# Opening of a fused adaLN, attention and GLU kernel: order of the modulation, activation and key weight loads, and of the products on them

## The chip, the cores and the metric

The kernel runs on one core of a Trainium2 chip. Its engines run side by side, each through its own list of instructions in order: TensorE (PE; its weight loads are shown apart as PEld), VectorE (DVE), ScalarE (ACT), GpSimd (POOL) and SyncE (SP). Loads and stores are issued as DMAs, here mostly from SP's queue and a few from ScalarE's, and all are carried by 16 DMA engines. The metric is device time in microseconds for one execution, as the median of several runs. The profile comes from one further execution with the hardware profiler.

## The reference

One block of a transformer on x of 2048 x 512, with a condition vector c of 512:

```python
mod = (_silu(c) @ w_mod).reshape(c.shape[0], 6, 1, -1)
sa, ca, ga, sb, cb, gb = (mod[:, 0], mod[:, 1], mod[:, 2], mod[:, 3], mod[:, 4], mod[:, 5])
h = _layernorm(x, axis=-1) * (1 + ca) + sa
x = x + ga * _A_ref(h, A_wq, A_wk, A_wv, A_wo, A_beta)
h = _layernorm(x, axis=-1) * (1 + cb) + sb
x = x + gb * _B_ref(h, B_w_gate, B_w_up, B_w_down)
```

`_A_ref` is attention with 32 heads of 16 over four segments of 512 rows: a softmax inside each segment, and a linear memory (`M`, `z`) that is carried from one segment to the next. `_B_ref` is a bilinear GLU with a hidden width of 1376. Everything is float32.

## The kernel before

The rows of x are taken in four segments of 512, each in four tiles of 128 rows (t). The 512 columns are four blocks of 128 (d or k). PE multiplies in a rounded float32 format, so each operand is split into a high part and a low part (names end in H and L), and a product is made of three: high by high, low by high, high by low. Splitting takes an operation on ScalarE or VectorE for the high part and a subtraction on VectorE or GpSimd for the low part.

The change lies in the opening, before the first attention scores. What happens there:

- **Condition.** `s_c` gets c (line 628, on SP's queue), ScalarE takes an exponential (`e`, line 670), and three small VectorE operations make the gate silu(c). `be` is beta, loaded on ScalarE's queue.
- **x.** `xload(0)` loads four tiles (`x`, line 643). The generator `ln` makes statistics on VectorE (`ast`, `amv`), a reciprocal root with ScalarE (`asd`, `ay`), normalises the four tiles in place (VectorE, `x<-x,amv,ay`), transposes them on PE into four banks (`atp`, one for each d), and then for each d scales and shifts with the modulation on ScalarE (`ahf`) and splits (`ahH`, `ahL`). For d = 0 and 2 the high part is made on VectorE (a cast), for d = 1 and 3 on ScalarE; all low parts are VectorE's.
- **Modulation.** `w_mod` columns for shift and scale (sa, ca) are loaded as eight blocks of 256 KB: `wm0_load(j)` loads half j of the columns for the four blocks k of the condition. Half 0 serves d = 0 and 1, half 1 serves d = 2 and 3. `mod0(j)` multiplies the four blocks of a half by the gate on PE (`m<-s_c,wm`; 16 matmuls in the program, which the trace shows as 32 records), and `mod0_out(j)` copies the result to `modc` on VectorE. The `ahf` of d = 0, 1 waits for the first copy, that of d = 2, 3 for the second.
- **Warm-up.** `warm(n)` issues n matmuls on zeros (`wups<-wu`), so that PE is at work before its data is there. `wu` is filled by VectorE.
- **Weights.** `load_g` loads the key or query weights of a group of eight heads (`wrk`, `wrq`) and splits them; `load_v` does so for the value weights (`wrv`). For the first group the high part is made on ScalarE, the low part on VectorE.
- **Projections.** `a_kq(0, 0, "k")` and `a_kq(0, 0, "q")` make the key and query products of the first group, 12 matmuls each (`kps`, `qps`). They are generators that pause after every third matmul, and the code alternates between them: six of one, six of the other for the blocks k = 0, 1, and then for k = 2, 3 as the activation blocks come in. The value products (`vps`) follow.

Order is written by hand: PE's instructions are chained in the order of the calls (`MM`, `TP`), a call of `pin` ties another engine's instruction or a DMA behind the last PE instruction of the program order for the scheduler, and the objects `CV` and `CA` chain VectorE and ScalarE in the opening. Loads on SP's queue stand in the order of their calls. Each DMA gets one of eight completion counters in turn, those issued from ScalarE's queue included, and it waits for the DMA that used its counter before.

The lines that drive the opening (1100 on):

```python
lw = [load_g("k", wk_, 0), load_g("q", wq, 0), load_v()]
next(lw[0])
wm0_load(1)
next(lw[1])
next(lw[2])
lng = ln(pa, pa, xts.pop(0), 0, ca_c, sa_c, "a", ("h", 8, 2), True)
next(lng)
mod0(0)
next(lng)
mod0_out(0, mp0[0])
mod0(1)
```

Of the kernel before, what the change touches and what calls it, by code (L numbers as in the profile page):

```python
# [8 lines left out]
F32 = mybir.dt.float32  # L9
# [8 lines left out]
P = 128  # L18
S, D, H, DH, NSEG, L, F = 2048, 512, 32, 16, 4, 512, 1376
KT = D // P  # L20
# [37 lines left out]
def tile_kernel(ctx, tc, x, wq, wk_, wv, wo, beta, w_gate, w_up, w_down, c, w_mod, out):  # L58
    nc = tc.nc
# [3 lines left out]
    def open_pool(**kw):  # L63
        p = tc.tile_pool(**kw)
        return p, p.__enter__()
# [13 lines left out]
    def pin(i):  # L79

        if last_pe[0] is not None:
            tc.add_manual_dep(i.ins, last_pe[0].ins.name, NOSYNC, reason="order")

    def MM(*a, **k):
        return pe(nc.tensor.matmul(*a, **k))  # L85
# [31 lines left out]
    def flush():  # L117

        while later:
            later.pop(0)()  # L120
# [36 lines left out]
    s_c = cst.tile([P, KT], F32, name="s_c")  # L157
# [9 lines left out]
    def rows(s, t):  # L167
        return slice(s * L + t * P, s * L + (t + 1) * P)
# [80 lines left out]
    apool, ap = open_pool(name="ap", bufs=1)  # L249
    PT = 6  # L250
# [374 lines left out]

    pwpool, pw = open_pool(name="pw", bufs=1, reuse_waits="tile")
    papool, pa = open_pool(name="pa", bufs=2, reuse_waits="tile")
    nc.sync.dma_start(s_c, c)
    wm = w_mod.rearrange("(k p) n -> p k n", p=P)

    def load_mod(i):
# [7 lines left out]
    def xload(s):  # L639
        xt = []  # L640
        for t in range(4):
            a = pa.tile([P, D], F32, tag="x", name=f"x{s}_{t}", bufs=4)
            pin(nc.sync.dma_start(a, x[rows(s, t), :]))
            xt.append(a)
        return xt

    xts = {0: xload(0)}
    NWU = 20
    wu = pa.tile([P, 512], BF, tag="rl", name="wu", bufs=1)
    vec.memset(wu, 0.0)  # L650
    wups = psp.tile([P, 2, 512], F32, tag="lk", name="wups", bufs=1)
# [1 line left out]
    def warm(n):  # L653
        for i in range(n):
            MM(wups[:, 0], wu[:, 0:P], wu, start=True, stop=True)

    warm(NWU)
    wm0 = []
    for k in range(KT):
        a = ap.tile([P, 2, 2, 256], F32, tag="pt", name=f"wm0_{k}", bufs=PT)  # L660
        wm0.append(a)

    def wm0_load(j):
        for k in range(KT):
            pin(nc.sync.dma_start(wm0[k][:, j], wm[:, k, :].rearrange("p (i c) -> p i c", c=D)[:, 0:2, 256 * j:256 * j + 256]))

    wm0_load(0)
    r0 = [[a[:, j].rearrange("p i c -> p (i c)") for a in wm0] for j in range(2)]
    nc.scalar.dma_start(be, beta[None, :].to_broadcast([P, H]))
    act.activation(e1, s_c, AF.Exp, scale=-1.0)  # L670
# [45 lines left out]
        CV.tensor_copy(sa_c[:, 2 * j:2 * j + 2], ps[:, 0:2])  # L716
        CV.tensor_scalar_add(ca_c[:, 2 * j:2 * j + 2], ps[:, 2:4], 1.0)

    def mod0(j):
        ps = mp0[j].rearrange("p (i n) -> p i n", n=P)[:, :, 0:MW]  # L720
        for k in range(KT):
            for i in range(4):
                MM(ps[:, i], r0[j][k][:, i * P:(i + 1) * P], s_c[:, k:k + 1].to_broadcast([P, MW]),
                   start=k == i == 0, stop=k == KT - 1, skip_group_check=True)
# [18 lines left out]
    wH, wL = {}, {}  # L743
# [3 lines left out]
    def staged(nm):  # L747
        tg, n = stage[nst[0] % len(stage)]
        nst[0] += 1
        return (ap if tg == "memb" else pa).tile([P, D], F32, tag=tg, name=f"wr{nm}", bufs=n)  # L750

    def load_g(nm, w, g):

        A, V = CA if g < 2 else act, CV if g == 0 else nc.gpsimd
        raw = staged(f"{nm}{g}")
        hi = wH[nm, g] = pw.tile([P, KT, P], F32R, tag=f"w{nm}H{g}", name=f"w{nm}H{g}", bufs=1)
        lo = wL[nm, g] = pw.tile([P, KT, P], F32R, tag=f"w{nm}L{g}", name=f"w{nm}L{g}", bufs=1)
        pin(nc.sync.dma_start(raw.rearrange("p (k c) -> p k c", c=P),
                              w.rearrange("(k p) n -> p k n", p=P)[:, :, g * P:(g + 1) * P]))
        yield  # L760
        hi, lo = (a.rearrange("p k (d h) -> p k h d", h=HG) for a in (hi, lo))
        raw = raw.rearrange("p (k h d) -> p k h d", k=KT, h=HG)
        pin(A.activation(hi, raw, AF.Copy))
        V.tensor_sub(lo, raw, hi.bitcast(F32))
        yield

    def load_v():
        raws = []
        for k in range(KT):
            wH["v", k] = pw.tile([P, D], F32R, tag=f"wvH{k}", name=f"wvH{k}", bufs=1)  # L770
            wL["v", k] = pw.tile([P, D], F32R, tag=f"wvL{k}", name=f"wvL{k}", bufs=1)
            raws.append(staged(f"v{k}"))
            nc.sync.dma_start(raws[k], wv[k * P:(k + 1) * P, :])
        yield
        for k in range(KT):
            CA.activation(wH["v", k], raws[k], AF.Copy)
            CV.tensor_sub(wL["v", k], raws[k], wH["v", k].bitcast(F32))
            yield
# [20 lines left out]
    def a_kq(s, g, nm):  # L799

        hH, hL = hcur[0]
        ph = phs.setdefault((s, g), {})
        if True:
            dst = kd if nm == "k" else qd
            ps = bank(f"{nm}ps{s}_{g}")
            n = 0
            three = ((wH, hH), (wH, hL), (wL, hH)) if s == 0 and g < 2 else ((wH, hH), (wL, hH), (wH, hL))
            terms = [(k, *ab) for k in range(KT) for ab in three]
            if s == 0 and g == 1:
                terms.sort(key=lambda t: t[1] is wL)  # L810
# [12 lines left out]
            A.activation(q3[:, i0, :], f, AF.Copy)  # L823
            V.tensor_sub(r, f, q3[:, i0, :])

            def rest():
                (CV.tensor_copy if fast else act.copy)(q3[:, i1, :], r)
                V.tensor_sub(q3[:, i2, :], r, q3[:, i1, :])
                nc.sync.dma_start(dst[s][g].rearrange("r p t -> p r t"), q3)

            if fast:
                rest()
            phi = (nm == "k" and s < NSEG - 1) or (nm == "q" and s > 0)
            if phi:
                if fast:
                    yield 0.0
                if nm == "q" and g > 0:
                    yield from drain()
                e = pa.tile([P, L], F32, tag="ph", name=f"ph{nm}{s}_{g}", bufs=3)
                if behind or after:  # L840
                    settle()
                rl = pa.tile([P, L], F32, tag="rl", name=f"rl{nm}{s}_{g}", bufs=1)
                ph[nm] = e

                def feature():
                    for a, fn in ((rl, AF.Relu), (e, AF.Exp)):
                        i = (CA if fast else act).activation(a, f, fn)
                        if lastex[0] is not None:
                            tc.add_manual_dep(i.ins, lastex[0].ins.name, NOSYNC, reason="order")

                def feature2():
                    pin((CV if fast else vec).scalar_tensor_tensor(e, e, 1.0, rl, op0=ALU.min, op1=ALU.add))
# [26 lines left out]
    def drain():  # L879
        while memq:  # L880
            w = mem_step()
            if w is not None:
                yield w
# [214 lines left out]
            credit[0] -= (mem_step() if len(key) == 3 and memq else next(fa)) or 0.0  # L1098

    lw = [load_g("k", wk_, 0), load_g("q", wq, 0), load_v()]  # L1100
    next(lw[0])
    wm0_load(1)
    next(lw[1])
    next(lw[2])
    lng = ln(pa, pa, xts.pop(0), 0, ca_c, sa_c, "a", ("h", 8, 2), True)
    next(lng)
    mod0(0)
    next(lng)
    mod0_out(0, mp0[0])
    mod0(1)  # L1110
    next(lw[0])
    next(lng)
    next(lng)
    mod0_out(1, mp0[1])
    next(lw[1])
# [433 lines left out]
    for f, tag in ((0, "bh7"), (1, "bl7"), (LAST, "bh4")):  # L1549
        a = pc.tile([P, 2, L], F32, tag=tag, name=f"q0_{f}", bufs=1)  # L1550
# [53 lines left out]
    for n in range(NU):  # L1604
        p, nm, i = units[n]
# [69 lines left out]
```

## Time and profile before

| what | us |
|---|---|
| median of 3 runs | 855.8 |
| lowest and highest run | 855.62, 856.07 |
| the profiled execution, its own time | 855.95 |
| its span in the trace | 854.2 |
| PE busy / VectorE busy / ScalarE busy | 835.8 / 642.2 / 498.0 |
| PE idle in the span (854.2 - 835.8) | 18.4 |

The granted clock of PE is 1.00 throughout. In a timeline each row is a start, a duration, the engine, the line, the operation with the tiles it writes and reads, and, in brackets, how long the engine was idle before it and what ended that. "SPq" and "ACTq" are DMA issues on these queues: their duration is that of the issue, not of the transfer. Line 39 and line 85 are helpers through which most operations of the opening go, so the tile's name tells one from another. A matmul's duration reaches past the start of the next one, since they are pipelined: what one costs in a row of many is the distance between starts.

### The profile page before, as it was taken

The numbers are of one execution on the slowest core, as the hardware profiler recorded it, in microseconds if no ns is written. First come the engines' busy times: TensorE is split into PE (matmuls) and PEld (weight loads), VectorE is DVE, ScalarE is ACT, GpSimd is POOL, SyncE is SP. The second block draws the span as 40 slices with busy tenths as digits, with TensorE's granted clock in tenths as the row PEclk, the third lists the DMA queues.
The fourth block names the chain that finished last, engine by engine and source line by source line (L and its number), as shares of the span: only waits on it lengthen the run. The fifth ranks groups of instructions, "written<-read, shape, count | busy, mean of one in ns | idle before, by whom it ended". The sixth has DMA issues, their size and how long they took to land.

```text
span 854.2 us, 14419 instructions
## 1 busy us (share of the span) xinstructions
PE 835.8 (98%) x4982; PEld 598.2 (70%) x4982; DVE 642.2 (75%) x1796; ACT 498.0 (58%) x759; POOL 276.2 (32%) x423
## 2 busy tenths in 40 slices
PE   9989999999999999999999999999999999999998
PEld 6756656666665656656665677887888778888886
DVE  7897768887778967787888359999987855447554
ACT  4758767787676876677545626344445546455230
POOL 2756627566565764675434600000000000000000
PEclk9999999999999999999999999999999999999999
DMA  8655435564545554456674456588650675335102
GB/s 271 153 151 157 119 105 143 157 178 117 139 110 169 144 166 102 123 160 219 200 215 148 149 176 220 198 281 286 242 201 33 229 269 213 126 136 185 40 11 98
DMA packets 83928, 139.57 MB, mean 163 GB/s; under 512 B 12720, under 2 KB 46768, under 8 KB 83856
## 3 DMA queue, kind: packets, MB, share of 16 engines
q1 hardware_dynamic: 83568, 138.52, 51.9%
q8 instruction: 39, 0.64, 0.3%
q14 instruction: 33, 0.27, 0.1%
q10 hardware_dynamic: 288, 0.15, 0.1%
HBM read 89.87 MB, written 48.50 MB: 162 GB/s over the span
## 4 chain that ended last, share of the span: by engine, by line
PE 60%; DVE 4%; ACT 2%; POOL 2%; issue 1%; DMA 0%; DVEq 0%; POOLq 0%; ACTq 0%
PE acc L1351 14%; PE Xu L1282 7%; PE Xg L1282 7%; PE wops L85 5%; PE tb L85 4%; PE Yu L1282 4%; PE Yg L1282 4%; PE k L85 3%; PE q L85 3%; DVE q L39 2%; PE Zg L1282 1%; PE Zu L1282 1%; PE qps L85 1%; PE vps L85 1%; PE ctp L88 1%; PE Xx L1282 1%
## 5 line engine op out<-in xcount | busy, mean ns | idle before, releaser
L39 DVE CUSTOM_DVE_ANT_0 q<-q,cmask 128x384 f32<-128x384 f32 (+3 forms) x512 | 248.2, 503 | 72.5 <-PE q L85 64.8
L335 ACT ACTIVATE pt<-k 128x1024 f32<-128x1024 f32 x160 | 164.0, 1025 | 74.1 <-PE k L85 72.1
L341 POOL TENSOR_SCALAR_AFFINE_SELECT pt<-pt 128x256 f32<-128x256 f32 (+1 forms) x224 | 97.9, 451 | 138.0 <-ACT pt L335 137.5
L85 PE MATMUL q<-kst,qst 96*128 96x384 bf16 (+3 forms) x512 | 122.8, 302 | 6.4 <-DVE nm L39 5.5
L85 PE MATMUL k<-qst,kst 98*128 98x384 bf16 (+3 forms) x512 | 95.9, 299 | 1.6 <-ACT pt L335 1.3
L1359 DVE TENSOR_TENSOR xa<-xa,acc 128x512 f32<-128x512 f32 x95 | 64.7, 683 | 40.0 <-PE acc L1351 38.1
L85 PEld LDWEIGHTS <-qst 96*128 96x128 bf16 x512 | 43.9, 98 | 57.9 <-issue 42.7
L85 PE MATMUL tb<-pt,v 128*32 128x512 f32 (+3 forms) x1024 | 75.8, 436 | 0.3 <-POOL pt L341 0.3
L39 DVE DVE_READ_ACCUMULATOR2_ANT nm<- 128x1 f32 x512 | 71.9, 140 | 0.0
L85 PEld LDWEIGHTS <-kst 98*128 98x128 bf16 x512 | 44.5, 98 | 25.0 <-issue 8.8
L1351 PE MATMUL acc<-dH,mH 128*128 128x512 f32 (+1 forms) x152 | 60.3, 397 | 0.0
L1351 PE MATMUL acc<-dL,mH 128*128 128x512 f32 (+1 forms) x152 | 60.1, 395 | 0.0
L1351 PE MATMUL acc<-dH,mL 128*128 128x512 f32 (+1 forms) x152 | 60.0, 395 | 0.0
L85 PEld LDWEIGHTS tb<-pt,v 128*32 128x32 f32 x1024 | 28.6, 109 | 39.1 <-issue 35.4
L367 ACT ACTIVATE tsb<-tb 128x512 f32<-128x512 f32 x32 | 19.1, 596 | 31.6 <-PE tb L85 31.5
L1351 PEld LDWEIGHTS acc<-dL,mH 128*128 128x128 f32 (+1 forms) x152 | 28.6, 188 | 7.1
L1351 PEld LDWEIGHTS acc<-dH,mL 128*128 128x128 f32 (+1 forms) x152 | 28.5, 188 | 7.1 <-DVE mL L1302 0.3
L1351 PEld LDWEIGHTS acc<-dH,mH 128*128 128x128 f32 (+1 forms) x152 | 28.5, 188 | 6.7
L85 PE MATMUL kps<-ahH,wkH 128*128 128x512 f32 x64 | 29.4, 460 | 0.0
L85 PE MATMUL wops<-woH,oH 128*128 128x512 f32 x64 | 28.3, 442 | 0.7 <-ACT oH L530 0.7
L85 PE MATMUL qps<-ahH,wqH 128*128 128x512 f32 x64 | 28.7, 448 | 0.0
L85 PE MATMUL vps<-wvH,ahH 128*128 128x512 f32 x64 | 28.3, 442 | 0.0
(399 smaller groups left out, 2018.5 us busy)
## 6 DMA issues: line engine op xcount, KB each, us to landing
wm<-in_w_mod_dram SPq DMA_DIRECT2D x24, 256.0 KB, 4.3
kd<-k SPq DMA_DIRECT2D x16, 384.0 KB, 2.5
qd<-q SPq DMA_DIRECT2D x16, 384.0 KB, 3.2
kst<-kd SPq DMA_DIRECT2D x32, 192.0 KB, 3.2
qst<-qd SPq DMA_DIRECT2D x32, 192.0 KB, 3.6
x<-in_x_dram SPq DMA_DIRECT2D x16, 256.0 KB, 4.6
kst<-kd SPq DMA_DIRECT2D x32, 128.0 KB, 3.1
qst<-qd SPq DMA_DIRECT2D x32, 128.0 KB, 3.6
```

The source lines that it names most:

```text
L39: i = getattr(self.eng, name)(*a, **k)
L85: return pe(nc.tensor.matmul(*a, **k))
L88: return pe(nc.tensor.transpose(*a))
L335: ex = act.activation(pt, kp, AF.Exp, scale=0.25)
L341: sels[u, i] = nc.gpsimd.affine_select(w, w, pattern=[[0, w.shape[1]], [1, P]], compare_op=ALU.is_ge, fill=0.0, base=0, channel_multiplier=-1)
L367: act.activation(tsbs[u], tbs.pop(u), AF.Copy)
L1282: pe(nc.tensor.matmul(ps[0:n], a, b[:, k], start=first and c == 0, stop=last and c == 5, skip_group_check=True))
L1351: pe(nc.tensor.matmul(ps, a[0:m, t * P:(t + 1) * P], b[0:m], start=j == 0, stop=j == n - 1))
L1359: vec.tensor_add(xa, xa, ps)
```

## The change

It touches the opening alone.

- The condition is loaded on ScalarE's queue, ahead of beta, and no longer on SP's.
- `wm0_load` and `mod0` take the blocks k that they are to handle. Blocks 0 and 1 of half 0 are loaded first of all, then x, then blocks 2 and 3 of half 0, then blocks 0 and 1 of half 1, then the key weights, then blocks 2 and 3 of half 1.
- Eight warm-up matmuls come first, then the products with blocks 0 and 1 of half 0, then ten more warm-up matmuls, then the products with blocks 2 and 3 of half 0 and 0 and 1 of half 1, then the transposes of x, then the products with blocks 2 and 3 of half 1.
- The products of the first key and query group are sorted: of the two blocks k = 0, 1 the four with the high weights come first and then the two with the low weights, and so again for k = 2, 3.

```diff
-    nc.sync.dma_start(s_c, c)
+    nc.scalar.dma_start(s_c, c)
...
-    xts = {0: xload(0)}
-    NWU = 20
...
-    warm(NWU)
     wm0 = []
     for k in range(KT):
         a = ap.tile([P, 2, 2, 256], F32, tag="pt", name=f"wm0_{k}", bufs=PT)
         wm0.append(a)
 
-    def wm0_load(j):
-        for k in range(KT):
+    def wm0_load(j, ks=range(KT)):
+        for k in ks:
             pin(nc.sync.dma_start(wm0[k][:, j], wm[:, k, :].rearrange("p (i c) -> p i c", c=D)[:, 0:2, 256 * j:256 * j + 256]))
 
-    wm0_load(0)
+    wm0_load(0, (0, 1))
+    xts = {0: xload(0)}
+    wm0_load(0, (2, 3))
...
+    warm(8)
...
-    def mod0(j):
+    def mod0(j, ks=range(KT)):
         ps = mp0[j].rearrange("p (i n) -> p i n", n=P)[:, :, 0:MW]
-        for k in range(KT):
+        for k in ks:
...
-            if s == 0 and g == 1:
-                terms.sort(key=lambda t: t[1] is wL)
+            if s == 0 and g < 2:
+                terms.sort(key=lambda t: (t[0] // 2 if g == 0 else 0, t[1] is wL))
...
     lw = [load_g("k", wk_, 0), load_g("q", wq, 0), load_v()]
+    wm0_load(1, (0, 1))
     next(lw[0])
-    wm0_load(1)
+    wm0_load(1, (2, 3))
     next(lw[1])
     next(lw[2])
     lng = ln(pa, pa, xts.pop(0), 0, ca_c, sa_c, "a", ("h", 8, 2), True)
+    mod0(0, (0, 1))
+    warm(10)
     next(lng)
-    mod0(0)
+    mod0(0, (2, 3))
+    mod0(1, (0, 1))
     next(lng)
     mod0_out(0, mp0[0])
-    mod0(1)
     next(lw[0])
     next(lng)
+    mod0(1, (2, 3))
     next(lng)
```

On SP, from its first load on, the rows were these (s_c is the condition, x_0 to x_3 the tiles of x, wm_0 to wm_3 the modulation blocks of the four k, wrk and wrq the first key and query weights; numbers at the end of a name are buffers):

```order
L628 DMA s_c<-in_c_dram 128x4
L643 DMA x_0_202<-in_x_dram 128x512
L643 DMA x_1_204<-in_x_dram 128x512
L643 DMA x_2_206<-in_x_dram 128x512
L643 DMA x_3_208<-in_x_dram 128x512
L665 DMA wm_0_233<-in_w_mod_dram 128x2x256
L665 DMA wm_1_234<-in_w_mod_dram 128x2x256
L665 DMA wm_2_235<-in_w_mod_dram 128x2x256
L665 DMA wm_3_236<-in_w_mod_dram 128x2x256
L758 DMA wrk_252<-in_wk_dram 128x4x128
L665 DMA wm_0_233<-in_w_mod_dram 128x2x256
L665 DMA wm_1_234<-in_w_mod_dram 128x2x256
```

and are now these:

```order
L654 DMA wm_0_202<-in_w_mod_dram 128x2x256
L654 DMA wm_1_203<-in_w_mod_dram 128x2x256
L643 DMA x_0_208<-in_x_dram 128x512
L643 DMA x_1_210<-in_x_dram 128x512
L643 DMA x_2_212<-in_x_dram 128x512
L643 DMA x_3_214<-in_x_dram 128x512
L654 DMA wm_2_204<-in_w_mod_dram 128x2x256
L654 DMA wm_3_205<-in_w_mod_dram 128x2x256
L654 DMA wm_0_202<-in_w_mod_dram 128x2x256
L654 DMA wm_1_203<-in_w_mod_dram 128x2x256
L758 DMA wrk_242<-in_wk_dram 128x4x128
L654 DMA wm_2_204<-in_w_mod_dram 128x2x256
```

The condition has left the queue, x stands two modulation blocks further back from the front, and the key weights stand behind ten blocks where they stood behind eight blocks and the condition.

On PE, the end of the warm-up and the modulation products before the transposes were these (m is a half's result, wups the warm-up's):

```order
L85 LDWEIGHTS wu
L85 MATMUL wups<-wu 128x512
L85 MATMUL m_250<-s_c,wm_0_233 128x96 x4
L85 MATMUL m_250<-s_c,wm_1_234 128x96 x4
L85 MATMUL m_250<-s_c,wm_2_235 128x96 x4
L85 MATMUL m_250<-s_c,wm_3_236 128x96 x4
L88 MATMUL atp_0_319<-ident,x_0_202 128x128
```

and now, from the end of the second warm-up on, this:

```order
L85 LDWEIGHTS wu
L85 MATMUL wups<-wu 128x512
L85 MATMUL m_238<-s_c,wm_2_204 128x96 x4
L85 MATMUL m_238<-s_c,wm_3_205 128x96 x4
L85 MATMUL m_239<-s_c,wm_0_202 128x96 x4
L85 MATMUL m_239<-s_c,wm_1_203 128x96 x4
L88 MATMUL atp_0_325<-ident,x_0_208 128x128
```

The same number of products stands ahead of the transposes, but two of them belong to the second half; the two that left this place, blocks 0 and 1 of the first half, stand between the two bursts of warm-up.

On PE, the key products of k = 0, 1 were these:

```order
L85 MATMUL kps_0_379<-ahH_0_365,wkH_253 128x512
L85 MATMUL kps_0_379<-ahL_0_366,wkH_253 128x512
L85 MATMUL kps_0_379<-ahH_0_365,wkL_254 128x512
L85 MATMUL kps_0_379<-ahH_1_371,wkH_253 128x512
L85 MATMUL kps_0_379<-ahL_1_372,wkH_253 128x512
L85 MATMUL kps_0_379<-ahH_1_371,wkL_254 128x512
```

and are now these:

```order
L85 MATMUL kps_0_377<-ahH_0_355,wkH_243 128x512
L85 MATMUL kps_0_377<-ahL_0_356,wkH_243 128x512
L85 MATMUL kps_0_377<-ahH_1_369,wkH_243 128x512
L85 MATMUL kps_0_377<-ahL_1_370,wkH_243 128x512
L85 MATMUL kps_0_377<-ahH_0_355,wkL_244 128x512
L85 MATMUL kps_0_377<-ahH_1_369,wkL_244 128x512
```

The low weights (wkL) moved from the third and sixth place to the fifth and sixth, and the low part of the second activation block (ahL_1) from the fifth to the fourth. VectorE's and ScalarE's order of operations stays the same, apart from the condition's load on ScalarE.

More of the change, by code (lines that the diff above doesn't have):

```diff
@@ L645, in xload @@
         return xt
+    wm0 = []
+    for k in range(KT):
+        a = ap.tile([P, 2, 2, 256], F32, tag="pt", name=f"wm0_{k}", bufs=PT)
+        wm0.append(a)
+    def wm0_load(j, ks=range(KT)):
+        for k in ks:
+            pin(nc.sync.dma_start(wm0[k][:, j], wm[:, k, :].rearrange("p (i c) -> p i c", c=D)[:, 0:2, 256 * j:256 * j + 256]))
+    wm0_load(0, (0, 1))
     xts = {0: xload(0)}
-    NWU = 20
+    wm0_load(0, (2, 3))
     wu = pa.tile([P, 512], BF, tag="rl", name="wu", bufs=1)
@@ L655, in warm @@
             MM(wups[:, 0], wu[:, 0:P], wu, start=True, stop=True)
-    warm(NWU)
-    wm0 = []
-    for k in range(KT):
-        a = ap.tile([P, 2, 2, 256], F32, tag="pt", name=f"wm0_{k}", bufs=PT)
-        wm0.append(a)
-    def wm0_load(j):
-        for k in range(KT):
-            pin(nc.sync.dma_start(wm0[k][:, j], wm[:, k, :].rearrange("p (i c) -> p i c", c=D)[:, 0:2, 256 * j:256 * j + 256]))
-    wm0_load(0)
+    warm(8)
     r0 = [[a[:, j].rearrange("p i c -> p (i c)") for a in wm0] for j in range(2)]
@@ L717, in mod0_out @@
         CV.tensor_scalar_add(ca_c[:, 2 * j:2 * j + 2], ps[:, 2:4], 1.0)
-    def mod0(j):
+    def mod0(j, ks=range(KT)):
         ps = mp0[j].rearrange("p (i n) -> p i n", n=P)[:, :, 0:MW]
-        for k in range(KT):
+        for k in ks:
             for i in range(4):
```

## The prediction

> **What bounds the kernel now.** I read the page's first part, then the timeline of each engine over the first 60 us, where every edit lies, then a windows row for what comes behind. The columns of a timeline are start, duration, engine, line, operation, tiles and, in brackets, the idle time before it with what ended it.
>
> ```profile
> span 854.2 us, 14419 instructions
> PE 835.8 (98%) x4982; PEld 598.2 (70%) x4982; DVE 642.2 (75%) x1796; ACT 498.0 (58%) x759; POOL 276.2 (32%) x423
> ```
>
> PE is busy nearly throughout, so a microsecond is won or lost only where PE does something the result doesn't need, or waits. The opening is such a place:
>
> ```profile
> 1.69 6.39 PE L85 MATMUL wups<-wu 128*128 128x512 bf16 x20 [1.69 <-DVE wu L650]
> 8.31 3.78 PE L85 MATMUL m<-s_c,wm 128*128 128x96 f32 x32 [0.23 <-DMA wm<-in_w_mod_dram]
> 11.93 1.91 PE L88 MATMUL atp<-ident,x 128*128 128x128 f32 x16
> 13.67 3.71 PE L85 MATMUL m<-s_c,wm 128*128 128x96 f32 x32
> 17.17 0.48 PE L85 MATMUL kps<-ahH,wkH 128*128 128x512 f32 x1
> ...
> 22.83 0.39 PE L85 MATMUL vps<-wvH,ahH 128*128 128x512 f32 x1
> ```
>
> Up to 8.08 PE only multiplies zeros to stay warm. Then come the two halves of the modulation (m, 32 records each, 0.114 us apart: 11.93 - 8.31 = 3.62 over 32), the 16 transposes of x between them (1.74), and from 17.17 the 24 key and query products (22.83 - 17.17 = 5.66, or 0.235 each). From there to the first attention scores PE has no gap:
>
> ```profile
> 22.80:36.00 13.20, 13.20 (x58) 1.00 0.71 160
> ```
>
> (stretch, its length, PE busy and matmul count, granted clock, DMA share, GB/s). So what the change moves the start of vps by, the rest should move by. That start, 22.83, is the quantity I follow; the key projection's end, from which ScalarE, VectorE and the stores of k go on, lies at a fixed 0.7 ahead of it (three query products of 0.235).
>
> Who feeds the opening is seen on SP, VectorE and ScalarE:
>
> ```profile
> 0.82 0.39 SPq L628 DMA_DIRECT2D s_c<-in_c_dram  x1
> 1.26 1.85 SPq L643 DMA_DIRECT2D x<-in_x_dram  x4
> 5.42 0.37 SPq L758 DMA_DIRECT2D wrk<-in_wk_dram  x1
> 7.46 0.37 SPq L665 DMA_DIRECT2D wm<-in_w_mod_dram  x1
> 8.19 0.37 SPq L665 DMA_DIRECT2D wm<-in_w_mod_dram  x1
> 8.96 0.37 SPq L758 DMA_DIRECT2D wrq<-in_wq_dram  x1
> 9.71 0.65 SPq L773 DMA_DIRECT2D wrv<-in_wv_dram  x1
> 11.37 0.33 SPq L773 DMA_DIRECT2D wrv<-in_wv_dram  x1
> ```
>
> A load waits until the one eight before it (beta's on ScalarE's queue counts) has landed, so late issues are landing times: 5.42 is x_0, 7.46 x_3, 8.19 the first modulation block, 8.96 the second, 9.71 the third, 11.37 the key weights. A block of x takes (7.46 - 5.42)/3 = 0.68, one of the modulation 0.76. Loads of 256 KB each come one behind the other; the transfer rate, not the issue, spaces them.
>
> ```profile
> 4.39 0.21 ACT L670 ACTIVATE e<-s_c 128x4 f32<-128x4 f32 x1 [2.30 <-DMA s_c<-in_c_dram]
> 4.76 0.23 ACT L680 ACTIVATE omg<-be 128x32 f32<-128x32 f32 x1 [0.15 <-DMA be<-in_beta_dram]
> 5.05 0.16 DVE L39 TENSOR_TENSOR s_c<-s_c,e 128x4 f32<-128x4 f32 x1
> 5.43 0.69 DVE L39 BATCH_NORM_STATS2 ast<-x 128x6 f32<-128x512 f32 x1 [0.22 <-DMA x<-in_x_dram]
> 10.12 1.91 DVE L39 TENSOR_SCALAR x<-x,amv,ay 128x512 f32<-128x512 f32 x4
> 11.38 1.15 ACT L39 ACTIVATE wkH<-wrk 128x512 fp32r<-128x512 f32 x1 [2.09 <-DMA wrk<-in_wk_dram]
> 13.55 1.45 ACT L39 ACTIVATE ahf<-atp,modc 128x512 f32<-128x512 f32 x2 [1.02 <-PE atp L88]
> 15.56 1.12 ACT L39 ACTIVATE wqH<-wrq 128x512 fp32r<-128x512 f32 x1
> 15.69 0.69 DVE L39 TENSOR_TENSOR ahL<-ahf,ahH 128x512 fp32r<-128x512 f32 x1 [0.18 <-ACT ahH L39]
> 17.42 0.16 DVE L39 COPY modc<-m 128x2 f32<-128x2 f32 x1 [1.04 <-PE m L85]
> 17.57 1.22 DVE L39 TENSOR_TENSOR wqL<-wrq,wqH 128x512 fp32r<-128x512 f32 x1
> 17.74 1.45 ACT L39 ACTIVATE ahf<-atp,modc 128x512 f32<-128x512 f32 x2 [1.05 <-DVE modc L39]
> 18.66 0.47 DVE L39 CAST ahH<-ahf 128x512 fp32r<-128x512 f32 x1
> 25.69 1.21 ACT L39 ACTIVATE wkH<-wrk 128x512 fp32r<-128x512 f32 x1
> ```
>
> The reader is to see two idle times: VectorE (1.04) and ScalarE (1.05) wait just before 17.42 and 17.74 for the second modulation half. That half ends last before the second pair of activation blocks (ahf, ahH, ahL of d = 2, 3). PE's m products are the bound there, x is not.
>
> **The change, part by part.**
>
> *Loads.* The condition leaves SP's queue, so the first block is issued at 0.82 instead of 1.26: everything moves 0.44 earlier. Two modulation blocks go ahead of x: 2 x 0.76 = 1.52 later for x. Landings: modulation blocks 5.42 - 0.44 = 4.98 and 5.74; x_0 to x_3 at 6.42, 7.10, 7.78, 8.46; modulation blocks three to six 9.2, 10.0, 10.7, 11.5; key weights 12.3; the last two blocks 13.1 and 13.8; query weights 14.7. If the 0.44 isn't gained (the queue's start-up not shifting with the issue), all are 0.44 later; more than 0.44 isn't to be had from an issue slot of that length.
>
> *Condition.* On ScalarE's queue, ahead of beta. It landed by 4.39 on SP, beta on ScalarE's queue by 4.76: I take 4.4, the same bytes with nothing before them, and 4.76 as the late end. The finished gate s_c followed at 5.21 (5.05 + 0.16), so 5.2 to 5.6.
>
> *Warm-up and first products.* Eight warm-ups, not twenty, before the first m. Rows of two pairs of short windows give their spacing, early and late:
>
> ```profile
> 1.69 0.61 PE L85 MATMUL wups<-wu 128*128 128x512 bf16 x1 [1.69 <-DVE wu L650]
> 1.69 3.60 PE L85 MATMUL wups<-wu 128*128 128x512 bf16 x8 [1.69 <-DVE wu L650]
> ...
> 5.76 0.59 PE L85 MATMUL wups<-wu 128*128 128x512 bf16 x2
> 5.76 2.32 PE L85 MATMUL wups<-wu 128*128 128x512 bf16 x10
> ```
>
> (3.60 - 0.61)/7 = 0.427 us cold, (2.32 - 0.59)/8 = 0.216 warm. Ten of the twenty begin after 5.76, so the rate changed at about the ninth, 1.69 + 9 x 0.427 = 5.5. Eight end their slots at 1.69 + 8 x 0.427 = 5.11, so PE meets s_c with a gap of about 0.14. Sixteen m records: 5.25 + 16 x 0.114 = 7.1. Ten warm-ups: + 2.16 = 9.3. The next 32 m records need blocks landing at 9.2, 10.0, 10.7 and 11.5 and use them at 9.3, 10.2, 11.1, 12.0: no wait; end 12.95. Two warm-ups fewer in all cost nothing, since they lie before waiting time.
>
> *x.* VectorE's statistics start 6.42 instead of 5.43, and x is normalised 1.0 later, 11.1 to 13.0. Transposes follow m at 12.95; the fourth x is ready by 13.05, needed at 14.25, so PE and not x sets them. They end at 14.7 (13.67 before), ahf begins at 13.55 + 1.03 = 14.6. Sixteen last m records (blocks landed by 13.8) to 16.5. So kps can start at 16.5, 0.65 earlier than 17.17.
>
> *What takes it back.* The first pair of activation blocks is now 1.03 later: the second ahL ends at 15.69 + 0.69 + 1.03 = 17.4 and is wanted as fourth product at 16.5 + 3 x 0.235 = 17.2: PE waits 0.2. wqH follows at 16.6 to 17.7, wqL 17.75 to 18.95 (18.79 before), the ahH of d = 2 at 18.9 (18.66). ScalarE's second ahf starts at 17.75, as before, because the idle 1.05 is now used up. The ahL of d = 2 is ready near 20.1, wanted at 16.5 + 0.2 + 13 x 0.235 = 19.75: PE waits 0.35. Sum: 16.5 + 24 x 0.235 + 0.2 + 0.35 = 22.7, against 22.83: **-0.1 us**.
>
> *Reordered products, later key weights.* 24 matmuls either way. Key weights at 12.3 plus 1.15 for wkH and as much for wkL are ready by 14.7, three microseconds before wkL is first read (fifth product now). Cover gone, each microsecond of lateness would cost one; with 3 in hand I count 0. Putting the lo-weight products last lets PE reach ahL of d = 1 one product sooner than it is ready and gives later work to do meanwhile: the order moves the waits, the sum of the block is the same.
>
> *Behind wrk and the SP queue.* The loads of the next group's weights reuse x's buffers and so are issued only as the transposes free them, from 13.4 on, about 1.0 later. Blocks issued earlier keep the transfers busy then, and the first reader of these comes at 25.69, 12 us after. Without that cover the 1.0 would count in full; I count 0.
>
> The sum against the profiled execution (855.95 us, span 854.2, 1.75 around it): 854.1 + 1.75 = 855.85. That execution lies 0.15 over the median of the runs, 855.8, so against the median: **855.7**. Bounds: s_c early saves at most the 0.14 gap (-0.25 in all); s_c at 5.6 gives +0.25; the loads without the 0.44 also +0.25 (first block 5.42 and all behind it). Both ends together -0.25 to +0.5, that is 855.5 to 856.3; the scatter of runs adds 0.3.
>
> **Rivals.**
>
> *The clock is not granted in time (slower).* Before, PE ran 8 to 9 warm-ups at 0.427 and had 11 more in hand. Now the first burst ends just there, at 5.11, and the gap for s_c follows. If the release does not come by then, the ten later warm-ups cost 10 x (0.427 - 0.216) = 2.1 more, and sixteen m records between 0 more (they are paced by weight loads) and 16 x 0.114 = 1.8 more. PE sets the transposes, so this goes through in full: +2.0 to +3.8, about 858.7. For it: no margin. Against: busy time ahead of the first m is 3.4 us, near the 3.8 after which the rate changed, and m keeps PE nearly busy. It decides from the point where the early burst and the gap no longer count as steady work.
>
> The Trainium skill (TensorE: Matmul & The Clock Gate, Part 1) says that one busy window of about 3.4 us releases the clock, and that the windows run free of the kernel, so the point varies by half a microsecond. The rows, with 3.8 us, agree. As an estimate by that page, a burst of 3.42 us just fits one window, and a bad phase would hold the clock back by another 3.4 us, which is the case above.
>
> *The products don't run ahead of x at all.* The condition, small and shared with beta's slow transfer, lands at 5.0 or later. Then m starts near 5.9 and PE is 0.6 later from there through the transposes: +0.5, 856.2. For it: beta's 4.76. Against: beta is the larger transfer and now behind. No change that can be told.
>
> *A shifted phase frees the first attention units (faster).*
>
> ```profile
> 33.77 3.80 DVE L852 SCALAR_TENSOR_TENSOR phk<-phk,rlk 128x512 f32<-128x512 f32 x1 [1.02 <-ACT phk L847]
> 53.58 0.69 DVE L39 SCALAR_TENSOR_TENSOR phk<-phk,rlk 128x512 f32<-128x512 f32 x1
> 35.00:60.00 25.00, 22.11 (x119) 14.88 (x118) 23.38 (x79) 12.75 (x20) 16.37 (x18) 1.00 0.64 172
> ```
>
> One VectorE operation takes 3.80 where its like takes 0.69, beside GpSimd's work, and PE idles 2.9 in the 25 us after. If the overlap falls differently, up to 2.3 could come back: 853.4. Against: both engines start from the same key projection, so they move together.
>
> **How the numbers follow.** Forecast 0.58 (855.7), late condition 0.18 (856.2), late clock 0.14 (858.7), phase 0.10 (853.4). 0.2% is 1.7 us, about what a measurement tells from no change, so 854.1 to 857.5 counts as the same: 0.76; faster 0.10, slower 0.14. The range takes in the bounds and part of both rivals: 854.6 to 857.3.
>
> **What would show it.** First m at 5.2 to 5.6 and ten warm-ups spaced 0.216 right behind its sixteenth; x statistics at 6.4; transposes at 12.9 to 13.4; kps at 16.5 to 17.0 with two short PE waits on VectorE's ahL; vps within 0.4 of 22.83; VectorE's 3.80 operation unchanged and PE idle 2.9 in its 25 us. Wrong if warm-ups of the second burst are 0.427 apart, if m waits past 6, or if PE's idle time behind 36 us changes by more than one microsecond.

## The result, and the profile after

The changed kernel took 857.22 us (median of 21 runs, 856.24 to 858.77), the kernel before 855.92 beside it (21 runs, 855.51 to 856.91). The ratio is 1.0015, interval 1.0009 to 1.0021: slower by some 1.3 us, where no change was forecast. The profiled execution took 858.02, which is 0.8 over that median.

The page's first part, and the timeline of PE in the opening (start, duration, engine, line, operation, tiles, idle time before it and what ended that):

```profile
span 856.3 us, 14416 instructions
PE 836.1 (98%) x4980; PEld 597.8 (70%) x4980; DVE 642.0 (75%) x1796; ACT 497.9 (58%) x759; POOL 275.6 (32%) x423
```

```profile
1.69 3.45 PE L85 MATMUL wups<-wu 128*128 128x512 bf16 x8 [1.69 <-DVE wu L660]
4.97 1.03 PE L85 MATMUL m<-s_c,wm 128*128 128x96 f32 x8
6.50 1.13 PE L85 MATMUL m<-s_c,wm 128*128 128x96 f32 x8 [0.49 <-DMA wm<-in_w_mod_dram]
7.46 2.32 PE L85 MATMUL wups<-wu 128*128 128x512 bf16 x10
10.31 3.81 PE L85 MATMUL m<-s_c,wm 128*128 128x96 f32 x32 [0.53 <-DMA wm<-in_w_mod_dram]
13.96 1.91 PE L88 MATMUL atp<-ident,x 128*128 128x128 f32 x16
15.71 1.92 PE L85 MATMUL m<-s_c,wm 128*128 128x96 f32 x16
17.41 0.48 PE L85 MATMUL kps<-ahH,wkH 128*128 128x512 f32 x1
...
23.79 0.39 PE L85 MATMUL vps<-wvH,ahH 128*128 128x512 f32 x1
```

PE's busy time grew by 0.3 and the span by 2.1, so PE waits more. The value products start at 23.79 in place of 22.83: +0.96, where -0.1 was forecast. The start of kps, forecast at 16.5, is 17.41. Ahead of it stand two waits for modulation blocks that were not to be there (0.49, at 6.50, and 0.53, at 10.31). The first of them is one of the prediction's own signs of being wrong: m waits past 6.

SP's queue tells when the blocks landed. Here each of these issues waits for the counter of one earlier block, in the order of issue: 3.95 is the latest that the first modulation block can have landed, 6.47 is the second, 7.46 x_0, 8.14 x_1, 8.83 x_2, 9.53 x_3.

```profile
3.95 0.38 SPq L654 DMA_DIRECT2D wm<-in_w_mod_dram  x1
6.47 0.37 SPq L654 DMA_DIRECT2D wm<-in_w_mod_dram  x1
7.46 0.40 SPq L758 DMA_DIRECT2D wrk<-in_wk_dram  x1
8.14 1.05 SPq L654 DMA_DIRECT2D wm<-in_w_mod_dram  x2
8.83 0.37 SPq L654 DMA_DIRECT2D wm<-in_w_mod_dram  x1
9.53 0.37 SPq L758 DMA_DIRECT2D wrq<-in_wq_dram  x1
```

The first block is early (4.98 forecast), the second 0.7 late (5.74), and from x_0 on everything is 1.05 late at the forecast spacing (0.69). The loss lies in the 2.5 us between the first block and the second, forecast as 0.76, and in a further 0.3 up to x_0 (0.99 for 0.68).

What VectorE and ScalarE see of it:

```profile
3.79 0.20 ACT L670 ACTIVATE e<-s_c 128x4 f32<-128x4 f32 x1 [1.70 <-DMA s_c<-in_c_dram]
6.21 0.23 ACT L680 ACTIVATE omg<-be 128x32 f32<-128x32 f32 x1 [2.21 <-DMA be<-in_beta_dram]
7.47 0.69 DVE L39 BATCH_NORM_STATS2 ast<-x 128x6 f32<-128x512 f32 x1 [2.86 <-DMA x<-in_x_dram]
34.73 3.76 DVE L852 SCALAR_TENSOR_TENSOR phk<-phk,rlk 128x512 f32<-128x512 f32 x1 [1.04 <-ACT phk L847]
```

The condition came 0.6 earlier (3.79 for 4.39) and beta 1.45 later (6.21 for 4.76). Set beside each other, the windows of one microsecond of the kernel before and then of the change show why that matters (stretch, its length, PE, PEld, DVE, ACT and POOL busy with counts, granted clock, DMA busy share, GB/s):

```profile
2.00:3.00 1.00, 1.00 (x4) 0.36 (x3) 0.77 (x4) 0.09 (x1) 0.27 (x1) 1.00 0.42 35
3.00:4.00 1.00, 1.00 (x4) 0.40 (x3) 0.00 (x0) 0.00 (x0) 0.00 (x0) 1.00 0.54 154
4.00:5.00 1.00, 1.00 (x4) 0.30 (x2) 0.33 (x2) 0.43 (x2) 0.00 (x0) 1.00 0.96 259
5.00:6.00 1.00, 1.00 (x5) 0.41 (x4) 0.75 (x3) 0.00 (x0) 0.66 (x1) 1.00 0.99 371
```

```profile
2.00:3.00 1.00, 1.00 (x4) 0.36 (x3) 0.77 (x4) 0.09 (x1) 0.27 (x1) 1.00 0.78 193
3.00:4.00 1.00, 1.00 (x4) 0.40 (x3) 0.00 (x0) 0.20 (x1) 0.00 (x0) 1.00 0.74 217
4.00:5.00 1.00, 1.00 (x5) 0.46 (x3) 0.51 (x3) 0.00 (x0) 0.26 (x1) 1.00 0.90 100
5.00:6.00 1.00, 1.00 (x9) 0.84 (x7) 0.00 (x0) 0.00 (x0) 1.00 (x2) 1.00 0.73 224
```

The reader is to see the last two columns. Before, the transfers are slow up to 4 us and then reach their rate. In the change they begin well and then fall to 100 GB/s at 4 to 5 us, with the DMA engines 90% busy, and to 224 at 73% in the next. That is while beta's transfer is under way (its broadcast reads the same 128 bytes for each of 128 partitions). This gave the theory that the runs were to test, **B**: beta's transfer slows every block beside it, and the condition ahead of it on ScalarE's queue pushed it from the first microseconds onto the second modulation block and x.

### The profile page after: what moved, and what is told of

It is laid out like the page before. It is cut to its first block, busy times and chain, and to the rows that moved or that the text cites. A ratio compares the mean times of both kernels' runs of the same rounds, so it can differ in the third digit from the quotient of the medians.

```text
span 856.3 us, 14416 instructions
## 1 busy us (share of the span) xinstructions
PE 836.1 (98%) x4980; PEld 597.8 (70%) x4980; DVE 642.0 (75%) x1796; ACT 497.9 (58%) x759; POOL 275.6 (32%) x423
## 4 chain that ended last, share of the span: by engine, by line
PE 58%; DVE 5%; ACT 2%; POOL 2%; DMA 1%; issue 1%; SPq 0%; DVEq 0%; ACTq 0%; POOLq 0%
PE acc L1355 14%; PE Xg L1286 6%; PE Xu L1286 6%; PE wops L85 5%; PE tb L85 4%; PE Yu L1286 4%; PE Yg L1286 4%; PE k L85 3%; PE q L85 3%; DVE q L39 2%; PE Zg L1286 1%; PE Zu L1286 1%; PE qps L85 1%; PE vps L85 1%; ACT pt L335 1%
```

## The experiments

A common measure for all: when the sixth block of 256 KB has landed. In both orders the first six are the four of x and two of modulation, and SP's issue of wrq (in the runs with beta late too) waits for the sixth: 8.96 before, 9.53 in the change; 8.46 was forecast (x_3). Ratios are to the kernel before on the same chip, where its median was 855.85 to 856.07, so rows are best compared by their ratios (ten or eleven runs each, e7 four); "late" means beta loaded behind the first weights, "other rows" beta's load reading 128 different rows.

| run | order | condition on | beta | sixth block | vps | median | ratio [interval] |
|---|---|---|---|---|---|---|---|
| before | x first | SP | ScalarE | 8.96 | 22.83 | 855.92 | 1 |
| e4 | x first | ScalarE | ScalarE | 9.40 | 23.29 | 857.03 | 1.0012 [1.0003, 1.0021] |
| e10 | x first | SP | other rows | 8.45 | 22.85 | 855.64 | 0.9998 [0.9988, 1.0007] |
| e8 | x first | SP | late | 8.19 | 22.25 | 855.24 | 0.9989 [0.9980, 0.9998] |
| e11 | x first | ScalarE | late | 7.78 | 21.67 | 854.74 | 0.9987 [0.9977, 0.9996] |
| change | modulation first | ScalarE | ScalarE | 9.53 | 23.79 | 857.22 | 1.0015 [1.0009, 1.0021] |
| e5, the same | | | | 9.26 | 23.52 | 857.06 | 1.0012 [1.0003, 1.0021] |
| e6, old product order | | | | 9.00 | 23.40 | 857.12 | 1.0014 [1.0005, 1.0023] |
| e7, beta ahead of condition | | | | 9.09 | 27.42 | 859.68 | 1.0042 [1.0028, 1.0056] |
| e2 | modulation first | ScalarE | other rows | 7.92 | 22.43 | 856.97 | 1.0011 [1.0002, 1.0021] |
| e9, the same | | | | 8.46 | 22.71 | 856.76 | 1.0006 [0.9996, 1.0015] |
| e1 | modulation first | ScalarE | late | 8.23 | 22.88 | 856.28 | 1.0002 [0.9993, 1.0012] |
| e3 | modulation first | SP | ScalarE | 9.02 | 23.23 | 856.16 | 1.0003 [0.9994, 1.0012] |
| e14, the same | | | | 9.58 | 23.82 | 856.56 | 1.0009 [1.0000, 1.0019] |
| e12 | modulation first | SP | late | 9.42 | 23.68 | 857.01 | 1.0012 [1.0002, 1.0021] |
| e13, the same | | | | 9.42 | 23.67 | 856.88 | 1.0010 [1.0000, 1.0019] |

Landings and vps are of one profiled execution each; where a kernel ran twice they differ by up to 0.6 us, so a difference below that in one pair proves nothing.

### Beta out of the way (e1)

```diff
-    nc.scalar.dma_start(be, beta[None, :].to_broadcast([P, H]))
...
-        act.activation(omg, be, AF.Exp)
+        CA.activation(omg, be, AF.Exp)
...
     next(lw[2])
+    pin(nc.sync.dma_start(be, beta[None, :].to_broadcast([P, H])))
```

> The changed kernel with beta's load moved from ScalarE's queue to SP's, behind the value weights, and beta's second exponential placed behind the first. Theory B (beta's broadcast, 128 packets of 128 B that all read the same bytes, slows the blocks that are in transfer beside it; in the changed kernel that is the second modulation block and x_0): statistics of x_0 start near 6.4 instead of 7.47, vps near 22.8 instead of 23.79, time about 1.0 below the changed kernel. Theory F (the first block read from a tensor is slow whatever runs beside it, so x_0 is slow because w_mod was read first): x_0 stays at 7.4 to 7.5, vps at 23.8, time as the changed kernel within 0.3.

Rows of e1 (windows, SP, PE):

```profile
4.00:5.00 1.00, 1.00 (x3) 0.49 (x2) 0.50 (x3) 0.00 (x0) 0.31 (x1) 1.00 0.99 253
5.00:6.00 1.00, 1.00 (x6) 0.93 (x5) 0.00 (x0) 0.00 (x0) 1.00 (x2) 1.00 0.90 303
8.23 0.37 SPq L757 DMA_DIRECT2D wrq<-in_wq_dram  x1
9.48 3.71 PE L85 MATMUL m<-s_c,wm 128*128 128x96 f32 x32
16.48 0.48 PE L85 MATMUL kps<-ahH,wkH 128*128 128x512 f32 x1
22.88 0.39 PE L85 MATMUL vps<-wvH,ahH 128*128 128x512 f32 x1
```

The loss is gone: 856.28, ratio 1.0002, vps 22.88. B's size was right, and its rival (the first block of a tensor is slow by itself) doesn't explain the 0.9 that came back. No gain over the kernel before remains, though: e1 does what was forecast for the change (kps at 16.5, vps at 22.7).

### The same packets, other addresses (e2, e9, e10)

```diff
-    nc.scalar.dma_start(be, beta[None, :].to_broadcast([P, H]))
+    nc.scalar.dma_start(be, wo[0:P, 0:H])
```

> The changed kernel; beta's load reads 128 different rows of wo (32 columns each) instead of one row for all 128 partitions, so the head gates are computed from other numbers. Same packets, other addresses. Theory B with the shared address as its cause: x_0 statistics near 6.4, vps near 22.8. Theory B with the mere number of small packets as its cause, and theory F: x_0 at 7.4 to 7.5, vps at 23.8.

> The change with beta's load reading 128 different rows, once more (gates from other numbers), because its first trace was of the fastest of ten executions and doesn't fit their median. Theory B with the same address as the cause: the sixth block of 256 KB (the second of modulation and the four of x) lands near 7.9 us as in that trace, vps at 22.4 to 22.9. Rival N (128 small packets behind the condition on ScalarE's queue, whatever they read, hold up the blocks, and the first trace was an exception): sixth block at 9.0 to 9.5, vps 23.3 to 23.9, as in the change, which the median of 857 would fit.

> The kernel before with beta's load reading 128 different rows in place of one row 128 times, in its old place on ScalarE's queue; gates from other numbers. Same address: sixth block at 8.2 in place of 8.96, x_0 by 4.5, m from 8.08 (the warm-ups' end), vps near 22.5, ratio 0.9992 to 0.9998. Rival N: sixth block at 8.9 to 9.0, vps 22.8, ratio 1.000.

e2 and e9 are the change with this edit, e10 the kernel before. All three make the head gates from other numbers, so their outputs are not the reference's; only the times are of use. The windows of e2:

```profile
4.00:5.00 1.00, 1.00 (x4) 0.49 (x2) 0.40 (x3) 0.23 (x1) 0.40 (x1) 1.00 1.13 342
5.00:6.00 1.00, 1.00 (x9) 0.92 (x8) 0.59 (x1) 0.00 (x0) 1.00 (x2) 1.00 0.98 332
```

As many rows of the same length, at the same place in the queue, and the blocks run at 342 and 332 GB/s (293 and 291 in e9) where the change had 100 and 224. Sixth block: 7.92 and 8.46 against 9.00 to 9.53; in the kernel before 8.45 against 8.96. So it is reading one row 128 times that holds up the blocks, and not the number of small rows as such. Whether that lies in the shared address or in where beta stands in memory was not separated. The times follow only in part: e2 and e9 have vps 0.8 to 1.4 earlier than the change and e5, their medians are only 0.1 to 0.5 lower with overlapping intervals, and e2's trace was of the fastest of its ten executions. That part stays open. In e10 vps did not move although x_0 was ready at 4.11: the twenty warm-ups ended at 8.40 and held PE.

### One part of the change at a time (e3, e4)

e3 is the change with the condition back on SP's queue. e4 is the kernel before with this line alone:

```diff
-    nc.sync.dma_start(s_c, c)
+    nc.scalar.dma_start(s_c, c)
```

> The changed kernel with the condition back on SP's queue as first load; beta alone and first on ScalarE's queue as before the change. Theory B: beta's packets run beside the first modulation block again and are over before x_0, x_0 statistics near 6.9 (7.47 less about 1.0, plus 0.44 of issue), vps near 23.2, time 0.5 below the changed kernel. Theory F: everything 0.44 later than in the changed kernel, x_0 at 7.9, vps at 24.2, time 0.4 above it.

> The kernel before with the one edit that the condition is loaded on ScalarE's queue ahead of beta. Theory B: beta's packets come later and fall on x_1 to x_3, the first modulation product starts at 8.8 to 9.3 instead of 8.31, vps near 23.5 instead of 22.83, time 0.5 to 1.0 above the kernel before. Theory F: all blocks 0.44 earlier, first product at 8.1 (end of the warm-up), vps 22.6, time 0.2 below.

One line, with nothing else of the change, costs the kernel before 0.12% (e4, 857.03 against 856.07 in that batch). Its windows have the hole of the changed kernel:

```profile
3.00:4.00 1.00, 1.00 (x4) 0.39 (x3) 0.00 (x0) 0.20 (x1) 0.00 (x0) 1.00 0.98 189
4.00:5.00 1.00, 1.00 (x4) 0.29 (x2) 0.90 (x4) 0.00 (x0) 0.26 (x1) 1.00 0.34 97
5.00:6.00 1.00, 1.00 (x4) 0.36 (x3) 0.44 (x3) 0.00 (x0) 1.00 (x2) 1.00 0.50 178
```

x_0 itself is early there (statistics at 4.53); the blocks behind it pay, and the sixth lands at 9.40. Without that line the rest of the change measured 1.0003 (e3; 1.0009 when run again, e14), with x_0 at 7.00 and vps at 23.23 as B expected; but in e14 the sixth block came at 9.58 and vps at 23.82, no earlier than in the change.

### The move without beta (e8, e11)

e8 is the kernel before with beta late and 15 warm-ups for 20; e11 adds the condition's line to it.

```diff
-    NWU = 20
+    NWU = 15
...
-    nc.scalar.dma_start(be, beta[None, :].to_broadcast([P, H]))
...
+    pin(nc.sync.dma_start(be, beta[None, :].to_broadcast([P, H])))
```

> The kernel before with beta's load moved behind the modulation blocks and x on SP's queue, and 15 warm-ups for 20 (they would else end at 8.08 us and hide the gain); no part of the change in it. Theory B: without beta's transfer beside it x_0 lands 0.5 to 1 us earlier than 5.4, m starts at 7.3 to 7.8 in place of 8.31, vps at 21.9 to 22.4, and the time is 0.4 to 0.9 us below the kernel before, which would beat both kernels. Rival (the first microseconds of all loads are slow by themselves, so that beta costs nothing where it stood before): x_0 at 5.4, m at 8.3, no change.

> The kernel before with beta late, 15 warm-ups, and the condition alone on ScalarE's queue: against the run with beta late it has the condition's move and nothing else. Theory B (the move costs because it pushes beta): with no beta there the move is free, sixth block at 7.8 to 8.2 (the prediction's 0.44 gained, or not), vps 21.9 to 22.3, ratio 0.9984 to 0.9992. Rival C (the move itself costs 0.4): sixth block at 8.6, vps 22.7, ratio 0.9997.

Rows of e8 (SP and PE), and then of e11 (windows, SP, PE):

```profile
8.19 0.37 SPq L757 DMA_DIRECT2D wrq<-in_wq_dram  x1
1.69 6.26 PE L85 MATMUL wups<-wu 128*128 128x512 bf16 x15 [1.69 <-DVE wu L650]
7.79 3.71 PE L85 MATMUL m<-s_c,wm 128*128 128x96 f32 x32
22.25 0.40 PE L85 MATMUL vps<-wvH,ahH 128*128 128x512 f32 x1
```

```profile
4.00:5.00 1.00, 1.00 (x5) 0.36 (x3) 0.86 (x4) 0.04 (x1) 0.23 (x1) 1.00 1.04 336
5.00:6.00 1.00, 1.00 (x6) 0.43 (x5) 0.97 (x3) 0.00 (x0) 1.00 (x2) 1.00 0.99 361
7.78 0.37 SPq L757 DMA_DIRECT2D wrq<-in_wq_dram  x1
1.69 4.92 PE L85 MATMUL wups<-wu 128*128 128x512 bf16 x15 [1.69 <-DVE wu L650]
21.67 0.39 PE L85 MATMUL vps<-wvH,ahH 128*128 128x512 f32 x1
```

In the order of the kernel before, these settle the condition's line. With beta beside it, it costs 0.12% (e4); with beta away it costs nothing (0.9987 beside 0.9989). The traces say the same: the sixth block 0.44 later with beta (8.96 to 9.40), 0.41 earlier without (8.19 to 7.78), about the issue slot that the prediction counted on, though each pair alone is within the scatter of single traces. With the modulation ahead of x the line has the same two signs: from e3 to the change the median rises by 1.1 (0.7 from e14), from e12 and e13, without beta, to e1 it falls by 0.6 to 0.7. Both kernels beat the kernel before and the change; e11, at 854.74 and 0.9987 [0.9977, 0.9996], is the best version found, with nothing of the modulation ahead of x in it. No run has 15 warm-ups with beta in place; that they alone would not do it is argued from the trace of the kernel before, where PE waits 0.23 for the first modulation block after all twenty.

### The change again, the product order, and the queue's order (e5, e6, e7)

```diff
-            if s == 0 and g < 2:
-                terms.sort(key=lambda t: (t[0] // 2 if g == 0 else 0, t[1] is wL))
+            if s == 0 and g == 1:
+                terms.sort(key=lambda t: t[1] is wL)
```

> The change as it is, once more, so that one trace of it isn't taken for all. Theory B (beta's transfer, pushed onto the second modulation block and x_0): the statistics of x_0 again start 1.5 us or more after 5.43, vps starts at 23.3 to 24.0, and the ratio is 1.0012 to 1.0018. Theory S (the profiled execution was an odd one, and the slower median comes from scatter near 490 us): vps near 22.8 and the time still 1 us above that of the kernel before.

> The change with the key and query products of the first group in the order of the kernel before; all else as in the change. If the order moves waits and nothing else (the prediction's 0): vps within 0.2 us of the change's 23.8, ratio as the change's, near 1.0015. If the order is worth what it defers: wkL ends near 15.8 and is then read as third product at 17.9, which is no wait, but the ahL of d = 2 is read earlier by some products, so PE waits more there, at most 5 x 0.235 = 1.2 us, and vps starts as late as 24.9, ratio 1.0025.

e5 is the change itself and repeats its loss. With the old order of the products (e6, the diff above) vps is 23.40 beside 23.52, the median 857.12 beside 857.06: the order is worth nothing that the times show, as forecast (from kps to vps 6.53 pass in e6, 6.39 in e5). e7 swaps the two loads on ScalarE's queue:

```diff
-    nc.scalar.dma_start(s_c, c)
+    nc.scalar.dma_start(be, beta[None, :].to_broadcast([P, H]))
+    nc.scalar.dma_start(s_c, c)
...
-    nc.scalar.dma_start(be, beta[None, :].to_broadcast([P, H]))
```

> The change with the two loads on ScalarE's queue in the other order, beta ahead of the condition, and nothing else. Theory B: beta's transfer runs where it ran before, 1.9 to 4.5 us, beside the two modulation blocks, and x follows undisturbed at 0.68 a block: statistics of x_0 at 6.4 to 7.0, vps 22.9 to 23.3, time 0.4 to 1 us below the change. The condition, now behind beta, lands at 4.7 to 5.2 and m starts by 5.8. Rival T (two loads on ScalarE's queue in either order hold up the others, whichever is first): statistics of x_0 at 7.4, vps 23.8, time as the change's.

Both expectations missed, by much. Rows of e7:

```profile
6.38 0.20 ACT L670 ACTIVATE e<-s_c 128x4 f32<-128x4 f32 x1 [0.90 <-DMA s_c<-in_c_dram]
7.25 3.73 PE L85 MATMUL m<-s_c,wm 128*128 128x96 f32 x16 [1.97 <-DVE s_c L39]
10.77 3.42 PE L85 MATMUL wups<-wu 128*128 128x512 bf16 x10
```

Behind beta the condition lands at 6.4, two microseconds after it did on SP's queue. PE stands idle for 1.97, and what follows is slow: 16 records of m in 3.73 (2.01 in e5), ten warm-ups in 3.42 (2.32). The value products start at 27.42, and the kernel loses 0.42% (four runs).

### The corner that did not fit (e12, e13, e14)

e12 is e1 with the condition on SP's queue. By B it should have been as good as e1 or e8. It was not, so it ran once more beside e3's kernel.

> The change with beta late and the condition back on SP's queue: the two modulation blocks and their products ahead of x, and the new order of the products, are what is left of it. If only the loads' speed decides: sixth block at 8.2, x_0 at 6.0, vps 22.6 to 22.9, ratio 0.9995 to 1.000, as in the run of the change with beta late. Against the kernel before with beta late (vps 22.25) this prices the modulation ahead of x by itself: +0.4 to +0.6 by theory B, 0 by the prediction.

> The change with beta late and the condition on SP's queue, once more, beside the next run. Theory B (beta's transfer is what slows the blocks): the earlier trace was an exception, the sixth block lands at 8.2 to 8.7 and the time is no longer than that of the run with beta beside it. Theory M (the switch from modulation blocks to x has slow packets of its own, whatever beta does): sixth block at 9.0 to 9.5 again, vps 23.3 to 23.8, time 857.

> The change with the condition on SP's queue and beta in its place, once more. Theory B: sixth block near 9.0, vps 23.2, time 856.2 and 0.4 or more above the run without beta. Theory M: sixth block 8.9 to 9.5, the time within 0.3 us of the run without beta or below it.

Windows and landing in e13:

```profile
3.00:4.00 1.00, 1.00 (x4) 0.40 (x3) 0.33 (x2) 0.00 (x0) 0.51 (x1) 1.00 1.05 353
4.00:5.00 1.00, 1.00 (x4) 0.49 (x2) 0.00 (x0) 0.00 (x0) 1.00 (x2) 1.00 1.27 270
5.00:6.00 1.00, 1.00 (x7) 0.92 (x6) 0.00 (x0) 0.00 (x0) 1.00 (x2) 1.00 0.68 260
9.42 0.37 SPq L757 DMA_DIRECT2D wrq<-in_wq_dram  x1
```

Theory M holds here: with the modulation ahead of x and the condition on SP, the transfers sag to 260 to 270 GB/s at 4 to 6 us (227 and 260 in e12), when x follows the modulation blocks, though no beta is under way. The sixth block lands at 9.42 both times, 1.2 later than with x first (e8, 8.19), and the time is 0.10% to 0.12% above the kernel before. With beta in place it is no worse (9.02 and 9.58). So the modulation ahead of x has a cost of its own in this corner. e1, with the condition on ScalarE's queue, has a shallower sag (253 and 303 GB/s, where e11, with x first, has 336 and 361) and beside e11 it is later too: the sixth block by 0.45 (8.23 for 7.78), vps by 1.2 (22.88 for 21.67), the ratio 1.0002 for 0.9987. Not all of that is the loads': in e1 the m records at 9.48 follow eighteen warm-ups without a wait for a block, e11 has fifteen warm-ups, and no run parts the two. What makes these packets slow, and why the place of a 2 KB load decides it, was not found.

## Why the prediction was wrong

**The step that failed** is the first term of the sum, the landings: "The condition leaves SP's queue, so the first block is issued at 0.82 instead of 1.26: everything moves 0.44 earlier." The issue did move (0.81), and the transfers did begin sooner (193 GB/s at 2 to 3 us for 35). But the same line put the condition ahead of beta, so beta's transfer ran when the blocks were to be at their full rate. The prediction looked at beta only as something that might delay the condition ("beta is the larger transfer and now behind") and never asked what beta delays. The bound "if the 0.44 isn't gained" was taken as the worst case; the sixth block came not 0.44 earlier but 0.04 to 0.57 later (9.00 to 9.53 in three executions with these loads). With beta away the same order of loads and products lands as forecast or earlier (e1: x_0 at 6.13 for 6.42, the sixth block at 8.23 for 8.46), and vps comes at 22.88 for 22.7. A second error lies in the same term: 0.68 and 0.76 a block were taken from the steady part of the opening and applied to the first six, where a modulation block followed by x cost more even without beta (e12, e13). So beta's part is shown by runs; that it is the only part is not, since e12 and e13 lose nearly as much without it (1.0012 and 1.0010) and the medians of e2 and e9 hardly follow their landings.

That 857.22 still lies inside the stated range (854.6 to 857.3) is luck: the upper end was there for a late condition or a late clock, and neither came in the change.

**What it did to the sum.** kps at 17.41 for 16.5 is 0.9, the waits behind it 0.2: together the 1.1 by which 23.79 misses 22.7. The rest of the working stands in the main:

- First m came at 4.97, 0.3 before the 5.25 of the sum. The second burst at 0.216 (2.32 for ten) and PE setting the transposes: as written, each later by what the blocks were.
- From kps to vps 6.38 passed; less 24 x 0.235 = 5.64 that leaves 0.74 of waits, 0.55 forecast. Within it stand the two waits that were named, on the ahL of d = 1 and of d = 2.
- Products reordered: 0 (e6). Key weights and the next group's loads later: 0; behind vps VectorE runs 0.96 later (34.73 for 33.77), as vps does.
- The condition at 4.4: it came at 3.8, so the late-condition rival fell as put. e7 shows its mechanism alive, at another price: with beta ahead the condition is 2 us late, not 0.6.
- The late clock, 0.14: not in the change. In e7 it came, behind an idle PE, and the point from which it decides was named rightly (the early burst and the gap not counting as steady work). It came in part in e1 and e14 too: the first sixteen m records took 2.42 and 3.05 there, with no wait among them (2.01 in e5). The slow m of e7 took 1.7 more, near the upper of the two bounds put (0 and 1.8).
- The half microsecond by which the clock's point was to vary is too small: fifteen warm-ups took 4.92 in e11 and 6.26 in e8. The 1.34 between them, over 0.427 - 0.216, is six warm-ups more at the slow spacing, so as an estimate the point lies some 2.6 us apart.
- The shifted phase: the 3.80 operation is 3.76, and PE idles 2.85 in the 25 us from 36 on (2.89 from 35 on before).

The measured 1.3 is more than the 0.96 at vps. Behind vps the spans of the traces (span less vps) run from 831.1 (e3) to 832.6 (e13), without regard to the order of the loads; one trace each cannot tell what part of the remaining 0.3 belongs to the change.

The Trainium skill (DMA: Bandwidth & Descriptors, "Issuing engines are not separate DMA queues") says that loads from any engine end up on the same 16 DMA engines and interleave. The traces agree: beta's load on ScalarE's queue held the blocks of SP's queue to 100 GB/s at 4 to 5 us, and the other queue gave the condition another issue slot and no path of its own.

## What to carry to other kernels

A load that is moved takes its neighbours' times with it: ask of each transfer beside it not only when it lands but what it slows while it runs, and read the GB/s column for it: the DMA busy share alone does not show the hole (0.90 in the change, 0.34 in e4, at 100 and 97 GB/s). Try taking a small load that reads one row for all partitions out of a bandwidth-bound opening; here, with x first and fewer warm-ups, that gave the only gains (e8 and e11), while with the modulation first it took back the loss in one case (e1) and not in the other (e12, e13). And price the first few microseconds of loads from the rows of those microseconds, not from the steady spacing behind them.

## What the runs showed of the hardware

- Beside 128 reads of one 128-byte row, all loads together ran at about 100 GB/s for one microsecond and about 200 in the next (100 and 224 in the change, 97 and 178 in e4); beside 128 reads of different rows they did not (342 and 332 in e2, 293 and 291 in e9).
- The point at which PE's matmuls become fast varies from run to run under the same work: the fifteen warm-ups took 4.92 in e11 and 6.26 in e8, from the same start at 1.69. The Trainium skill (TensorE: Matmul & The Clock Gate, Part 1) has the deciding windows run free of the kernel, which would give such a scatter; the two rows show the scatter and not its cause.
- After an idle PE of 1.97 us right behind a cold burst, the next 16 records of m and part of the ten warm-ups behind them were slow (e7), though the column of the granted clock in its windows (third from the end) shows 1.00 there too. So the 1.00 of the pages says nothing of these first microseconds; the spacing of the matmuls tells more.

```profile
7.00:8.00 1.00, 0.75 (x3) 0.75 (x4) 0.93 (x5) 0.00 (x0) 0.68 (x1) 1.00 1.06 406
```
